# Attention scores on the two row halves of TensorE: head A on partitions 0-63, head B on 64-127

## The chip, the core and the metric

The kernel runs on one core of one Trainium2 chip. The metric is the time of one execution in device microseconds (us); for the kernel before, the median of three runs is 1126.16 us. Five engines work side by side and meet at semaphores: TensorE (PE in the profile, with PEld for its weight loads), VectorE (DVE), ScalarE (ACT), GpSimd (POOL) and SyncE (SP), which issues most DMA transfers.

## The reference

Three stages follow each other: an attention with a sigmoid in place of the softmax, a mixture of eight experts in which each token goes to the expert with the highest logit, and a feed-forward stage.

```python
scores = scale * np.matmul(q, k.transpose(0, 1, 3, 2)) - np.log(S)
attn = 1.0 / (1.0 + np.exp(-scores))
x = attn @ v                                     # 4 batches, 12 heads, S=448, D=64
logits = xn @ en.T / tau; expert = argmax(logits)
out[mask] = gate * (maximum(x[mask] @ w1[e], 0) @ w2[e])
h = out @ w_in;  result = (h - tanh(h)) @ w_out
```

The change touches only the scores of the attention.

## The kernel before

**Two parts for each float32.** Every large product is made from operands that are split into a high part in fp32r and the low rest, x = h + l, and summed from products of the parts.

**Units and slots.** Two heads, A and B, make a pair; there are 24 pairs, six for each batch. A unit is 128 keys by 448 queries of scores, put through the sigmoid and multiplied with v. 448 keys are three and a half times 128, so a pair has seven units: three of A, three of B, and one that holds the last 64 keys of A and of B. A slot is two units that follow each other; seven slots carry two pairs, and the middle one of the seven takes one unit of each pair. There are 84 slots, u = 0 to 83, and 21 of them make a batch.

**One slot.** `scores(u)` writes the two units into one of three PSUM buffers `pq` (two banks each). ACT reads it twice (L240 writes the high part `ah` of the sigmoid, L241 the full value back into `pq`), DVE subtracts (L242, `al`), and three slots later `av(u-3)` multiplies with v in three terms a unit (L255, six matmuls a slot). When all units of a pair are done, its result is copied (`xT`, L268 or L270) and `rows` turns it into token rows through a fourth user of the `pq` buffers (L280, `pr`).

**The scores before.** D is 64, so a head fills only 64 of the 128 partitions. The kernel therefore loads k and q twice, on partitions 0-63 and on 64-127 (`load`, L173). `prep` casts both (L192), then replaces q on the upper 64 partitions by its low part (L194, 64x448) and makes the low part of k (L196, 128x448). A matmul over 128 partitions then gives h·h and h·l at once, and a second one with k's low part gives the other two terms: two matmuls a unit, and four for the unit with the last keys, which takes A's and B's shares one after the other. That is 16 matmuls a pair. A and B have a tile each (`w[0]`, `w[1]`), so a pair has two casts, two L194 (A's on DVE, B's on POOL) and two L196 (POOL).

**What sets the order.** PE's program is written out by hand: scores(u), then av(u-3), then the events planned for slot u. `prep(i)` is planned for the slot after the last one of pair i-2, `load(i)` two slots after the last one of pair i-3, `rows(i)` five slots after the last one of pair i. The order on DVE, ACT, POOL and SP is made by a scheduler when the kernel is built; each engine then works its list strictly in order. `kq` has two buffers, so the load of pair i waits until DVE and POOL have read those of pair i-2.

**The end of the attention.** In batch 2 the routing of its tokens is planned eight slots after its rows, behind the scores of slot 75: `route_b` (L422, L424) ranks the tokens, POOL scatters the ids (L473), gathers ids and rows of the first group of tokens (L650, L654), ACT scales the rows (L658), and only after the rows does SP load the first expert's weights (L686), which ACT splits (L715) for the first matmuls of the experts (L725).

Of the kernel before, what the change touches and what calls it, by code (L numbers as in the profile page):

```python
# [10 lines left out]
F32 = mybir.dt.float32  # L11
F32R = mybir.dt.float32r
# [4 lines left out]
ALU = mybir.AluOpType  # L17
# [12 lines left out]
P = 128  # L30
# [4 lines left out]
def f32(ap):  # L35
    return ap.bitcast(F32)


class Prog:
# [87 lines left out]
    def attention(self):  # L127


        nc, tc = self.nc, self.tc  # L130
        B, H, S, D, NJ, E, R = self.B, self.H, self.S, self.D, self.NJ, self.E, self.R
        NP = H // 2
        HK = S - 3 * P
        cx = ExitStack()
        raw = self.pool("araw", 3, cx)
        sp = self.pool("asp", 3, cx)
        xp = self.pool("axp", 2, cx)
        pers = self.pool("apers", 1, cx)
        ps2 = self.pool("aps2", 3, cx, space=PSUM)
        self.ps1 = ps1 = ps2  # L140
        pav2 = self.pool("aps3", 2, cx, space=PSUM)

        self.ep = pers
        NV, NW = 2, 2
        ws, vhs, vls = [], [], []

        def wpads():
            for w in ws:
                for a, o in ((0, S), (1, 0)):
                    nc.gpsimd.memset(f32(w[a][:, 0::2, o : o + HK]), 0.0)  # L150

        def vpads():
            for i in range(NV):
                vh = pers.tile([P, 14, D], F32R, name=f"vh{i}")
                vl = pers.tile([P, 14, D], F32R, name=f"vl{i}")
                for t in (vh, vl):
                    nc.gpsimd.memset(f32(t), 0.0)
                vhs.append(vh)
                vls.append(vl)

        pairs = [(b, j) for b in range(B) for j in range(NP)]
        n = len(pairs)
        st = {}

        def load(i):

            b, j = pairs[i]
            kq = raw.tile([P, 2, 2, S], F32, tag="kq", name="kq", bufs=2)
            w = S if i == 0 else 2 * S
            for o in range(0, 2 * S, w):  # L170
                for t, src in ((1, self.q), (0, self.k)) if i == 0 else enumerate((self.k, self.q)):
                    for p0 in (0, D):
                        nc.sync.dma_start(  # L173
                            kq[p0 : p0 + D, t].rearrange("p a s -> p (a s)")[:, o : o + w],
                            src[b, j, :, o : o + w],
                        )
            vr = raw.tile([P, 2, 4, D], F32, tag="vr", name="vr")
            self.w_dma = nc.sync.dma_start(vr.rearrange("p h c d -> p (h c d)"), self.v[b, j])
            st[i] = dict(kq=kq, vr=vr)

        def prep(i):

            s = st[i]
            s["w"] = ws[i % NW]
            for a in range(2):
                kq = s["kq"][:, :, a]
                t = s["w"][a][:, :, a * HK : a * HK + S]
                if i == 0:
                    nc.vector.tensor_copy(t[:, 1], kq[:, 1])
                    nc.scalar.copy(t[:, 0], kq[:, 0])  # L190
                else:
                    nc.vector.tensor_copy(t[:, 0:2], kq)  # L192
                eng = nc.gpsimd if i and a else nc.vector
                eng.tensor_tensor(t[D:P, 1], kq[D:P, 1], f32(t[D:P, 1]), ALU.subtract)  # L194
                eng = nc.vector if i == 0 else nc.gpsimd
                eng.tensor_tensor(t[:, 2], kq[:, 0], f32(t[:, 0]), ALU.subtract)  # L196

        def prep_v(i):

# [6 lines left out]
            s["v"] = (vh, vl)  # L206


        units = []
        for i in range(n):  # L210
            units += [(i, 0, c * P, 8 + 2 * c) for c in range(3)]
            units += [(i, 2, 0, 6)]
            units += [(i, 1, (c + 1) * P, 2 * c) for c in range(3)]
        slots = [units[o : o + 2] for o in range(0, len(units), 2)]
        ns = len(slots)
        first = [7 * i // 2 for i in range(n)]
        final = [(7 * i + 6) // 2 for i in range(n)]
# [2 lines left out]
        def scores(u):  # L220
            hi = sp.tile([P, 2, S], F32R, tag="ah", name="ah", bufs=LAG + 2)
            lo = sp.tile([P, 2, S], F32R, tag="al", name="al", bufs=LAG + 2)
            tiles[u] = (hi, lo)
            pq = ps2.tile([P, 2, 512], F32, tag="qk", name="pq")
            for x, (i, a, c, _) in enumerate(slots[u]):
                w = st[i]["w"]
                ops = [(w[a], c)] if a < 2 else [(w[0], 3 * P), (w[1], 0)]
                m = 0
                for t, o in ops:
                    q = t[:, 1, :S] if t is w[0] else t[:, 1, HK:]  # L230
                    for z in (0, 2):
                        nc.tensor.matmul(  # L232
                            pq[:, x, :S], t[:, z, o : o + P], q, start=(m == 0), stop=(m == 2 * len(ops) - 1)
                        )
                        m += 1
            k = len(slots[u])
            pv = pq[:, :k, :S]
            sc = dict(bias=self.bias_s, scale=1.0 / math.sqrt(D))
            hi, lo = hi[:, :k], lo[:, :k]
            nc.scalar.activation(hi, pv, AF.Sigmoid, **sc)  # L240
            nc.scalar.activation(pv, pv, AF.Sigmoid, **sc)  # L241
            nc.vector.tensor_tensor(lo, pv, f32(hi), ALU.subtract)  # L242

        def av(u):
            hi, lo = tiles.pop(u)
            for x, (i, a, c, o) in enumerate(slots[u]):
                s = st[i]
                vh, vl = s["v"]
                if a == 0 and c == 0:
                    s["pav"] = pav2.tile([P, 512], F32, tag="av", name="pav")  # L250
                pav = s["pav"]
                vo = lambda t: t[:, o : o + 2].rearrange("p h d -> p (h d)")
                e = a == 1 and c == 3 * P
                for m, (vv, aa) in enumerate(((vh, hi), (vl, hi), (vh, lo))):
                    nc.tensor.matmul(  # L255
                        pav[:, :S], vo(vv), aa[:, x], start=(a == 0 and c == 0 and m == 0), stop=(e and m == 2)
                    )
                if e:
                    b, j = pairs[i]
                    if j == 0:  # L260
                        self.bts[b] = dict(
                            rec=xp.tile([CP, NCH, NJ * P], F32, tag="rec", name="rec"),
                            ss=self.sm.tile([CP, NCH], F32, tag="ss", name="ss"),
                            u=xp.tile([CP, NCH, E], F32, tag="u", name="u"),
                        )
                    s["xT"] = xp.tile([P, S], F32, tag="xT", name="xT")
                    if i % 2:
                        nc.scalar.copy(s["xT"], pav[:, :S])  # L268
                    else:
                        nc.vector.tensor_copy(s["xT"], pav[:, :S])  # L270
# [43 lines left out]

        self.bts = {}
        for i in range(NW):
            ws.append([pers.tile([P, 3, 512], F32R, name=f"w{i}{a}") for a in range(2)])
        wpads()
        vpads()
        with tc.high_priority():  # L320
            load(0)
            warm = self.cp.tile([P, 1], F32, name="warm")
            nc.scalar.activation(warm, self.bias_s, AF.Sigmoid)
        prep(0)
        for i in (1, 2):
            if i < n:
                load(i)
        if n > 1:
            prep(1)
        prep_v(0)  # L330
        pe = {mybir.EngineType.PE}
        with tc.manual_schedule(engines=pe):
# [29 lines left out]
            for i in range(n):  # L362
                if i >= 2:
                    plan(final[i - 2] + 1, prep, i)
                if i >= 3:
                    plan(final[i - 3] + 2, load, i)
                if i >= 1:
                    plan(first[i] + LAG - 2, prep_v, i)
                plan(final[i] + LAG + ROW + (3 if i == 0 else 0), rows, i)
                if pairs[i][1] == NJ - 1:  # L370
                    plan(final[i] + LAG + ROW, route, i)
            plan(5, self.embedding)
            now = [0]
            u = 0
            while u < ns + LAG:
                now[0] = u
                if u < ns:
                    scores(u)
                if LAG <= u < ns + LAG:
                    av(u - LAG)  # L380
                events(u)
                if u >= CONV:
                    conv()
                if u == ns and self.cv is not None:
                    for _ in self.cv:
                        pass
                u += 1
# [693 lines left out]
```

## Time and profile before

| what | value |
|---|---|
| median of 3 runs | 1126.16 us (1121.7 to 1127.59) |
| the profiled execution | 1122.56 us; span from first to last instruction 1120.8 us |
| PE busy over the span | 1030.4 us (92%), 6298 matmuls |
| DVE, ACT, POOL busy | 841.0 us (75%), 558.4 us (50%), 215.2 us (19%) |
| first sigmoid to routing of batch 2 | 10.40 us to 231.35 us |
| first matmul of the experts | 287.72 us |

The page gives busy time as an average over stages. A matmul of 448 columns is listed with some 365 ns, but the next one starts 0.20 us after it: matmuls overlap, and their starts, not their lengths, tell the rate. "[7.39 <-PE pq L232]" behind a row means that the engine sat idle for 7.39 us ahead of it and was released by line 232 on PE. "issue" stands where the profile names no releaser.

### The profile page before, as it was taken

How to read it: one execution, taken by the hardware profiler on the slowest of the kernel's cores; microseconds unless marked ns; L12 is line 12 of the kernel's file. 1: busy time of each engine (PE TensorE's matmuls, PEld its weight loads, DVE VectorE, ACT ScalarE, POOL GpSimd, SP SyncE). 2: the span in 40 equal slices, each digit the busy share in tenths (PEclk: the TensorE clock that was granted, in tenths of full speed). 3: DMA queues.
4: the chain of work that ended last, by engine and by line, in shares of the span. 5: the costliest groups of instructions: out<-in, count | busy, mean ns of one | idle time of the engine just before them, and what ended most of it. 6: DMA issues, size and time to landing. Idle time of an engine off the chain costs nothing. (4 is left out here: it accounts for less than half of the span.)

```text
span 1120.8 us, 16520 instructions
## 1 busy us (share of the span) xinstructions
PE 1030.4 (92%) x6298; PEld 980.6 (87%) x6298; DVE 841.0 (75%) x1136; ACT 558.4 (50%) x694; POOL 215.2 (19%) x218
## 2 busy tenths in 40 slices
PE   5998788892789999899999799999999999999996
PEld 4897687782779998899999799999999999999996
DVE  8999596790676977587888378888888666776674
ACT  4787576661556765566656353334435332233320
POOL 6666556451123111111000000000000210000002
PEclk8999899896799998899999899999999999999999
DMA  7675757606998899999683344454453442233312
GB/s 194 163 211 116 127 150 100 161 1 65 267 271 235 224 264 273 207 227 276 205 306 140 116 174 150 167 188 167 170 197 113 169 154 95 104 113 113 113 57 99
DMA packets 91800, 186.12 MB, mean 166 GB/s; under 512 B 13120, under 2 KB 64576, under 8 KB 91712
## 3 DMA queue, kind: packets, MB, share of 16 engines
q1 hardware_dynamic: 88064, 172.36, 54.6%
q0 software_dynamic: 3648, 12.61, 4.5%
q8 instruction: 52, 0.85, 0.3%
q14 instruction: 36, 0.29, 0.1%
HBM read 167.56 MB, written 36.26 MB: 182 GB/s over the span
## 5 line engine op out<-in xcount | busy, mean ns | idle before, releaser
L953 PE MATMUL o<-wo,gh 128*128 128x384 f32 x896 | 240.4, 335 | 0.7 <-DVE acc L963 0.7
L913 PE MATMUL z<-yh,wi 128*128 128x448 f32 x768 | 221.8, 371 | 6.0 <-ACT yh L888 6.0
L953 PEld LDWEIGHTS o<-wo,gh 128*128 128x128 f32 x896 | 162.9, 188 | 2.3 <-DVE acc L963 1.0
L913 PEld LDWEIGHTS z<-yh,wi 128*128 128x128 f32 x768 | 145.2, 190 | 18.4 <-ACT yh L888 6.2
L953 PE MATMUL o<-wo,gl 128*128 128x384 f32 x448 | 149.7, 334 | 0.0
L913 PE MATMUL z<-yl,wi 128*128 128x448 f32 x384 | 138.2, 368 | 0.0
L232 PE MATMUL pq<-w 128*128 128x448 f32 x384 | 101.8, 393 | 34.7 <-DVE al L242 22.5
L725 PE MATMUL pth<-xh,wh 128*128 128x256 f32 x432 | 124.3, 288 | 7.7 <-DVE hl L742 5.2
L725 PE MATMUL pty<-hh,wh 128*128 128x256 f32 x432 | 123.3, 290 | 6.1 <-ACT yT L758 4.1
L473 POOL DMA_INDIRECT out_dram<-acc,toki x14 | 17.3, 1232 | 578.6 <-DVE acc L963 578.6
L725 PE MATMUL pty<-hh,wl 128*128 128x256 f32 x432 | 123.6, 288 | 1.4 <-DVE wl L716 1.4
L725 PE MATMUL pth<-xl,wh 128*128 128x256 f32 x432 | 123.6, 286 | 0.0
L725 PE MATMUL pth<-xh,wl 128*128 128x256 f32 x432 | 123.3, 286 | 0.3 <-DVE wl L716 0.3
L725 PE MATMUL pty<-hl,wh 128*128 128x256 f32 x432 | 123.3, 287 | 0.0
L963 DVE TENSOR_TENSOR acc<-o,acc 128x768 f32<-128x768 f32 x98 | 93.5, 954 | 39.5 <-PE o L953 38.3
L240 ACT ACTIVATE ah<-pq,bias_s 128x896 fp32r<-128x896 f32 x84 | 85.0, 1012 | 66.3 <-PE pq L232 63.3
L232 PEld LDWEIGHTS pq<-w 128*128 128x128 f32 x384 | 73.4, 199 | 48.0 <-issue 32.2
L936 ACT CAST gh<-r 128x896 fp32r<-128x896 f32 x32 | 30.1, 941 | 158.7 <-DVE r L934 89.5
L242 DVE TENSOR_TENSOR al<-pq,ah 128x896 fp32r<-128x896 f32 x84 | 90.7, 1083 | 20.7 <-ACT pq L241 20.4
L716 DVE TENSOR_TENSOR wl<-w2raw,wh 128x1024 fp32r<-128x1024 f32 x54 | 66.2, 1225 | 34.2 <-ACT wh L715 33.3
L725 PEld LDWEIGHTS pth<-xh,wh 128*128 128x128 f32 x432 | 84.2, 195 | 8.2 <-issue 5.3
L725 PEld LDWEIGHTS pty<-hh,wh 128*128 128x128 f32 x432 | 84.0, 196 | 6.6 <-ACT yT L758 4.3
(199 smaller groups left out, 2206.0 us busy)
## 6 DMA issues: line engine op xcount, KB each, us to landing
w1raw<-in_moe_w_dram SPq DMA_DIRECT2D x36, 768.0 KB
w2raw<-in_moe_w_dram SPq DMA_DIRECT2D x27, 1024.0 KB
wi<-dwi SPq DMA_DIRECT2D x32, 768.0 KB
wo<-dwo SPq DMA_DIRECT2D x32, 768.0 KB
cr<-in_moe_w_in_dram SPq DMA_DIRECT2D x16, 768.0 KB
dwi<-cr SPq DMA_DIRECT2D x16, 768.0 KB
cr<-in_moe_w_out_dram SPq DMA_DIRECT2D x16, 768.0 KB
dwo<-cr SPq DMA_DIRECT2D x16, 768.0 KB
```

Of the source, the lines that this page charges most:

```text
L232: nc.tensor.matmul(pq[:, x, :S], t[:, z, o : o + P], q, start=(m == 0), stop=(m == 2 * len(ops) - 1))
L240: nc.scalar.activation(hi, pv, AF.Sigmoid, **sc)
L242: nc.vector.tensor_tensor(lo, pv, f32(hi), ALU.subtract)
L473: i = self.nc.gpsimd.indirect_dma_start(**kw)
L716: nc.vector.tensor_tensor(wl, cols, f32(wh), ALU.subtract)
L725: nc.tensor.matmul(pt[:, u], a[:, kk], b[:, kk], start=(n == 0), stop=(n == 3 * K - 1))
L913: nc.tensor.matmul(z[:, g, :GT], wi[:, a, j * P : (j + 1) * P], b[:, j], start=(n == 0), stop=(n == 3 * NJ - 1),)
L936: nc.scalar.copy(gv, r)
L953: nc.tensor.matmul(o[:, w, :NW], a[:, u, i * P : (i + 1) * P], wo[:, b, w * NW : (w + 1) * NW], start=(n == 0), stop=(n == 3 * CH - 1),)
L963: nc.vector.tensor_tensor(acc[i], ov, acc[i], ALU.add)
```

## The change

Head A lies on partitions 0-63 and head B on 64-127, each once. A tile `h` (high parts) and a tile `l` (low parts) hold, for both heads, 512 columns of k and 448 of q; the fourth block of 128 key columns is a block diagonal, with A's last 64 keys in its first 64 columns on the lower partitions, B's in its last 64 columns on the upper ones, and zeros elsewhere (`kpads` writes them once). A slot is now one A unit and one B unit with the same keys, and each unit is made of three matmuls over 64 partitions, h·h, h·l and l·h (the term l·l is left out), issued A, B, A, B, A, B. The middle slot of seven takes the block-diagonal unit of both pairs, three matmuls over all 128 partitions each. A pair has 18 matmuls over 64 partitions and 3 over 128. `prep` is one cast of 960 columns on DVE and two subtractions on POOL (448 and 512 columns). The load of a pair is five DMAs without copies, and `kq` has three fixed buffers in place of two.

```diff
-            kq = raw.tile([P, 2, 2, S], F32, tag="kq", name="kq", bufs=2)
...
+            kq = kqs[i % NK]
+            k, q = self.k[b, j], self.q[b, j]
+            for dst, src in (
+                (kq[:D, KW:], q[:, :S]),
+                (kq[D:, KW:], q[:, S:]),
+                (kq[:D, :S], k[:, :S]),
+                (kq[D:, : 3 * P], k[:, S + HK :]),
+                (kq[D:, S:KW], k[:, S : S + HK]),
+            ):
+                nc.sync.dma_start(dst, src)
...
-                    nc.vector.tensor_copy(t[:, 0:2], kq)
-                eng = nc.gpsimd if i and a else nc.vector
-                eng.tensor_tensor(t[D:P, 1], kq[D:P, 1], f32(t[D:P, 1]), ALU.subtract)
+                nc.vector.tensor_copy(h, kq)
+            for x in (qs, ks):
                 eng = nc.vector if i == 0 else nc.gpsimd
-                eng.tensor_tensor(t[:, 2], kq[:, 0], f32(t[:, 0]), ALU.subtract)
+                eng.tensor_tensor(l[:, x], kq[:, x], f32(h[:, x]), ALU.subtract)
...
+        slots = []
+        for i in range(0, n, 2):
+            ab = [[[(e, a, c * P, 8 * (1 - a) + 2 * c) for a in range(2)] for c in range(3)] for e in (i, i + 1)]
+            slots += ab[0] + [[(e, 2, 3 * P, 6) for e in (i, i + 1)]] + ab[1]
...
-                    for z in (0, 2):
-                        nc.tensor.matmul(
-                            pq[:, x, :S], t[:, z, o : o + P], q, start=(m == 0), stop=(m == 2 * len(ops) - 1)
-                        )
-                        m += 1
+            for m, (kt, qt) in enumerate(((0, 0), (0, 1), (1, 0))):
+                for x, (i, a, c, _) in enumerate(slots[u]):
+                    w = st[i]["w"]
+                    p = slice(0, P) if a == 2 else slice(a * D, (a + 1) * D)
+                    nc.tensor.matmul(
+                        pq[:, x, :S], w[kt][p, c : c + P], w[qt][p, KW:], start=(m == 0), stop=(m == 2)
+                    )
```

PE around slot 19, before: the last three products with v of slot 15, the rows of a pair, then the scores of slot 19 (`w_185` is A's tile, `w_186` B's, of pair 5; rows print the output's shape alone, so the height of a matmul in the array isn't seen).

```order
L255 MATMUL pav<-ah,vh_191 128x448
L255 MATMUL pav<-ah,vl_192 128x448
L255 MATMUL pav<-al,vh_191 128x448
L280 MATMUL pr<-ien,xT 112x136 x4
L232 MATMUL pq<-w_185 128x448 x2
L232 MATMUL pq<-w_186 128x448 x4
```

PE at the same place now (`w1h` and `w1l` are the high and low parts of pair 5).

```order
L253 MATMUL pav<-ah,vh_196 128x448
L253 MATMUL pav<-ah,vl_197 128x448
L253 MATMUL pav<-al,vh_196 128x448
L278 MATMUL pr<-ien,xT 112x136 x4
L230 MATMUL pq<-w1h 128x448 x2
L230 MATMUL pq<-w1l,w1h 128x448 x2
L230 MATMUL pq<-w1h,w1l 128x448 x2
```

Each "x2" is now A's matmul and B's with the same kind of term, on the two halves; every slot has six matmuls of scores where most had four.

DVE around slot 19, before: the subtractions `al` of slots 18 and 19 and, between them, the preparation of pair 7, with a cast for A, the low part of A's q, and a cast for B.

```order
L242 TENSOR_TENSOR al<-pq,ah 128x896
L192 CAST w_185<-kq 128x2x448
L194 TENSOR_TENSOR w_185<-kq,w_185 64x448
L192 CAST w_186<-kq 128x2x448
L242 TENSOR_TENSOR al<-pq,ah 128x896
L270 COPY xT<-pav 128x448
```

DVE at that place now, from `al` of slot 19 on.

```order
L239 TENSOR_TENSOR al<-pq,ah 128x896
L196 CAST w1h<-kq_188 128x960
L268 COPY xT<-pav 128x448
L207 CAST vh_196<-vr 128x4x64 x2
L239 TENSOR_TENSOR al<-pq,ah 128x896 x3
```

One cast is left of three operations; it waits for the last scores of the pair that used `w1h` before, and all of a pair's tile comes free at once, where A's came free ahead of B's.

More of the change, by code (lines that the diff above doesn't have):

```diff
@@ L143, in attention, with kpads @@
         self.ep = pers
[L144 to L150, printed above, removed]
+        NV, NW, NK = 2, 2, 3
+        KW = 4 * P
+        kqs, ws, vhs, vls = [], [], [], []
+        def kpads():
+            for t in kqs:
+                nc.vector.memset(t[:D, S:KW], 0.0)
+                nc.vector.memset(t[D:, 3 * P : S], 0.0)
         def vpads():
@@ L167, in load @@
             b, j = pairs[i]
-            kq = raw.tile([P, 2, 2, S], F32, tag="kq", name="kq", bufs=2)
[L169 to L175, printed above, removed]
-                        )
+            kq = kqs[i % NK]
[8 more added lines that the diff above has]
+                nc.sync.dma_start(dst, src)
             vr = raw.tile([P, 2, 4, D], F32, tag="vr", name="vr")
@@ L183, in prep @@
             s = st[i]
[L184 to L192, printed above, removed]
-                eng = nc.gpsimd if i and a else nc.vector
-                eng.tensor_tensor(t[D:P, 1], kq[D:P, 1], f32(t[D:P, 1]), ALU.subtract)
+            kq, (h, l) = s["kq"], ws[i % NW]
+            s["w"] = (h, l)
+            ks, qs = slice(0, KW), slice(KW, KW + S)
+            if i == 0:
+                nc.vector.tensor_copy(h[:, qs], kq[:, qs])
+                nc.scalar.copy(h[:, ks], kq[:, ks])
+            else:
+                nc.vector.tensor_copy(h, kq)
+            for x in (qs, ks):
                 eng = nc.vector if i == 0 else nc.gpsimd
-                eng.tensor_tensor(t[:, 2], kq[:, 0], f32(t[:, 0]), ALU.subtract)
+                eng.tensor_tensor(l[:, x], kq[:, x], f32(h[:, x]), ALU.subtract)
         def prep_v(i):
@@ L206, in prep_v @@
             s["v"] = (vh, vl)
[L209 to L214, printed above, removed]
+        slots = []
+        for i in range(0, n, 2):
+            ab = [[[(e, a, c * P, 8 * (1 - a) + 2 * c) for a in range(2)] for c in range(3)] for e in (i, i + 1)]
+            slots += ab[0] + [[(e, 2, 3 * P, 6) for e in (i, i + 1)]] + ab[1]
         ns = len(slots)
@@ L224, in scores @@
             pq = ps2.tile([P, 2, 512], F32, tag="qk", name="pq")
[L225 to L230, printed above, removed]
-                    for z in (0, 2):
-                        nc.tensor.matmul(
-                            pq[:, x, :S], t[:, z, o : o + P], q, start=(m == 0), stop=(m == 2 * len(ops) - 1)
-                        )
-                        m += 1
+            for m, (kt, qt) in enumerate(((0, 0), (0, 1), (1, 0))):
[5 more added lines that the diff above has]
+                    )
             k = len(slots[u])
@@ L248, in av @@
                 vh, vl = s["v"]
-                if a == 0 and c == 0:
-                    s["pav"] = pav2.tile([P, 512], F32, tag="av", name="pav")
+                if "pav" not in s:
+                    s["pav"], s["units"] = pav2.tile([P, 512], F32, tag="av", name="pav"), 0
                 pav = s["pav"]
                 vo = lambda t: t[:, o : o + 2].rearrange("p h d -> p (h d)")
-                e = a == 1 and c == 3 * P
+                b0, e = s["units"] == 0, s["units"] == 6
+                s["units"] += 1
                 for m, (vv, aa) in enumerate(((vh, hi), (vl, hi), (vh, lo))):
                     nc.tensor.matmul(
-                        pav[:, :S], vo(vv), aa[:, x], start=(a == 0 and c == 0 and m == 0), stop=(e and m == 2)
+                        pav[:, :S], vo(vv), aa[:, x], start=(b0 and m == 0), stop=(e and m == 2)
                     )
@@ L316, in attention @@
         for i in range(NW):
-            ws.append([pers.tile([P, 3, 512], F32R, name=f"w{i}{a}") for a in range(2)])
-        wpads()
+            ws.append([pers.tile([P, KW + S], F32R, name=f"w{i}{x}") for x in "hl"])
+        for i in range(NK):
+            kqs.append(pers.tile([P, KW + S], F32, name=f"kq{i}"))
+        kpads()
         vpads()
```

## The prediction, as it was written before the changed kernel ran

> **What bounds the kernel now.** I read the page first, for the span:
>
> ```profile
> span 1120.8 us, 16520 instructions
> ```
>
> The run took 1122.56 us, 1.8 us more than its span; the median of the three runs is 1126.16, so the profiled one is 0.3% below it, and I make the sum against 1122.56. Then the windows. The attention was cut at the sigmoids (L240) that open a batch of 21 slots, and the last piece starts at the routing of batch 2:
>
> ```profile
> core 0: us, PE busy (x) PEld busy (x) DVE busy (x) ACT busy (x) POOL busy (x), PEclk, DMA share, GB/s
> 10.40:66.96 56.56, 51.15 (x240) 44.31 (x240) 53.25 (x79) 42.23 (x48) 37.34 (x34) 0.94 0.71 189
> 66.96:122.00 55.04, 51.98 (x277) 47.20 (x276) 48.91 (x89) 43.69 (x56) 31.29 (x31) 1.00 0.68 133
> 122.00:186.26 64.26, 54.61 (x277) 48.66 (x276) 51.12 (x91) 43.93 (x56) 35.63 (x35) 0.95 0.67 135
> 186.26:231.35 45.09, 36.32 (x166) 31.82 (x164) 32.46 (x58) 27.86 (x38) 24.01 (x25) 0.89 0.51 134
> ```
>
> The second batch is the clean one: PE works 51.98 of 55.04 us, DVE 48.91, ACT 43.69. PE bounds it, with DVE close behind. What PE pays for a matmul is read from the starts in its timeline:
>
> ```profile
> 74.97 0.36 PE L255 MATMUL pav<-ah,vh 128*128 128x448 f32 x1
> 75.17 0.37 PE L255 MATMUL pav<-ah,vl 128*128 128x448 f32 x1
> 75.38 0.36 PE L255 MATMUL pav<-al,vh 128*128 128x448 f32 x1
> 75.58 0.97 PE L232 MATMUL pq<-w 128*128 128x448 f32 x4
> 76.39 0.36 PE L255 MATMUL pav<-ah,vh 128*128 128x448 f32 x1
> ```
>
> Seven starts in 1.42 us: 0.203 us each. The 96 score matmuls of a batch (16 for each of 6 pairs) are 19.5 us of PE.
>
> Batch three and the twelve slots behind it are slower than batch two, and the list of sigmoids shows one long gap in each, and a smaller one at the start:
>
> ```profile
> 10.40 1.01 ACT L240 ACTIVATE ah<-pq,bias_s 128x896 fp32r<-128x896 f32 x1 [4.47 <-PE pq L232]
> 14.49 1.01 ACT L240 ACTIVATE ah<-pq,bias_s 128x896 fp32r<-128x896 f32 x1 [1.74 <-PE pq L232]
> 135.83 1.01 ACT L240 ACTIVATE ah<-pq,bias_s 128x896 fp32r<-128x896 f32 x1 [7.39 <-PE pq L232]
> 199.06 1.01 ACT L240 ACTIVATE ah<-pq,bias_s 128x896 fp32r<-128x896 f32 x1 [7.51 <-PE pq L232]
> 230.40 1.01 ACT L240 ACTIVATE ah<-pq,bias_s 128x896 fp32r<-128x896 f32 x1 [2.12 <-PE pq L232]
> ```
>
> From the first row (slot 0) to the last (slot 75) are 75 slots. The first of the two long gaps, followed back:
>
> ```profile
> 124.80 1.14 POOL L196 TENSOR_TENSOR w<-kq,w 128x448 fp32r<-128x448 f32 x1
> 125.97 1.11 SPq L173 DMA_DIRECT2D kq<-in_k_dram  x2
> 132.13 0.63 DVE L192 CAST w<-kq 128x896 fp32r<-128x896 f32 x1 [6.26 <-DMA kq<-in_q_dram]
> 133.90 1.83 PE L232 MATMUL pq<-w 128*128 128x448 f32 x4 [5.27 <-DVE al L242]
> ...
> 195.36 0.63 DVE L192 CAST w<-kq 128x896 fp32r<-128x896 f32 x1 [6.34 <-DMA kq<-in_q_dram]
> ```
>
> POOL is done with `kq` at 125.94, the load of the pair two later goes out at 125.97, DVE sits in front of that pair's cast until 132.13, and `al`, which PE waits for, is queued behind the cast. The last row is the same wait in the second gap.
>
> Last, what follows slot 75:
>
> ```profile
> 231.35 0.19 PE L422 MATMUL prank<-oh,tri_b 112*128 112x32 bf16 x1
> 262.89 0.93 ACT L658 ACTIVATE xg<-xg 128x768 f32<-128x768 f32 x1 [12.60 <-DMA xg<-x_tok,gi]
> 286.83 1.56 ACT L715 CAST wh<-w1raw 128x768 fp32r<-128x768 f32 x2 [3.88 <-DMA w1raw<-in_moe_w_dram]
> ```
>
> From the routing at 231.35 a chain of scatters, gathers and weight loads runs 55.5 us to the experts' first cast, and ACT waits 12.60 us for the gathered rows; the last slots are done by then, or queued behind that wait. So a gain counts up to slot 75 alone, and moves everything behind it by as much. Of the 221 us ahead, that is 75/21 = 3.57 batches.
>
> **The change part by part.** *Scores on PE.* A batch has 54 pairs of half-height matmuls (9 for each of 6 pairs of heads) and 18 full ones, 3.65 us. What two halves cost together no row shows. They have 448 columns each, and PE's rate goes by columns (256 pass in 0.120 us in the next rows), so less than one full matmul, 0.203 us, is excluded: that is the lower end. If both run at once they still need two weight loads, and the experts' matmuls of 256 columns bring a load with each; behind them the lengths of this kernel's score matmuls and loads, and a load beside the matmul ahead of it:
>
> ```profile
> 400.05 0.28 PE L725 MATMUL pty<-hl,wh 128*128 128x256 f32 x1
> 400.17 0.28 PE L725 MATMUL pty<-hh,wl 128*128 128x256 f32 x1
> 400.29 0.28 PE L725 MATMUL pty<-hh,wh 128*128 128x256 f32 x1
> ...
> L232 PEld LDWEIGHTS pq<-w x384: 186/188/338, 8.3 to 249.8; 128*128 128x128 f32 x192
> L232 PE MATMUL pq<-w x384: 358/366/743, 8.3 to 250.0; 128*128 128x448 f32 x192
> ...
> 60.09 0.37 PE L255 MATMUL pav<-ah,vl 128*128 128x448 f32 x1
> 60.09 0.19 PEld L255 LDWEIGHTS pav<-al,vh 128*128 128x128 f32 x1
> ```
>
> A load and its matmul pass every 0.120 us, so two loads take at most 0.240 us. I take 0.22, between the two: 54 x 0.22 = 11.9, with the full ones 15.5 us, 4.0 less than 19.5. The Trainium skill (TensorE: Matmul & The Clock Gate, Part 3 on packing small matmuls) models tiles on different rows as running at once, a few ns apart; a pair would then be an estimated 0.207 us and the sum 1093. No row of this case shows it.
>
> *Changes of height.* 18 of 21 slots now go from full height (products with v) to half and back, 36 changes a batch. If the array runs on, each costs 0; if the next matmul can start only when the last has left, it costs what a matmul lasts beyond its pace, 0.366 - 0.203 = 0.163 us. A gain has no reason. Nothing is nearer to either end, so I take half, 0.08: 2.9 us. PE's net is -1.1 us a batch, x 3.57 = -3.9 us.
>
> *Preparation.* The operations of the second batch:
>
> ```profile
> L192 DVE CAST w<-kq 128x896 fp32r<-128x896 f32 x12 | 8.0, 669 | 2.2 <-PE pav L255 2.0
> L194 DVE TENSOR_TENSOR w<-kq,w 64x448 fp32r<-64x448 f32 x6 | 5.9, 991 | 0.2
> L196 POOL TENSOR_TENSOR w<-kq,w 128x448 fp32r<-128x448 f32 x10 | 11.5, 1149 | 5.9 <-DVE w L192 5.5
> PE pq L232 <- DVE al L242: 3.0, 3, 2.1
> PEld pq L232 <- DVE al L242: 0.9, 1, 0.9
> ```
>
> DVE loses 8.0 + 5.9 and gains six casts of 960 columns, by length 0.72 us each, 4.3: 9.6 of its 48.91 us go. PE's waits for `al` in this batch are 3.9 us. All could go or none; PE's own pace holds some slots to the same time. I take half, 1.95 x 3.57 = -7.0 us, between 0 and -13.9. On POOL two subtractions a pair, 1.15 and by length 1.31 us, take the place of three. The new cast waits for the last scores of pair i-2, with `al` of the next slot queued behind it, but that `al` needs the same scores through ACT, so the wait costs nothing. Cast and subtractions are 0.72 + 1.15 + 1.31 = 3.2 us; three slots at 55.04/21 = 2.6 us each cover them. Were that cover gone, PE would wait the rest, up to 3 us a pair.
>
> *Loads.* The third `kq` buffer ties a load to the pair three before, one pair (3.5 slots, 9 us) earlier than now, against a wait of 6.26; and a pair is half the data:
>
> ```profile
> kq<-in_k_dram SPq DMA_DIRECT2D x46, 224.0 KB
> ```
>
> Four such DMAs a pair were 896 KB, now 448. SP issues six DMAs a pair with v's in place of five, some 0.6 us each (1.11 for two above), 3.5 us in 9. Both long gaps should go: -7.4 - 7.5 = -14.9 us; what is late next is PE itself. At the start head B's separate preparation (the 1.74) goes too: -1.7. The six memsets of `kpads` come before the first `kq` lands, when DVE is idle (0.87 us in the next row), and the ones on POOL go; if they took longer than that, some tenths.
>
> ```profile
> 4.14 3.36 DVE L189 CAST w<-kq 128x448 fp32r<-128x448 f32 x1 [0.87 <-DMA kq<-in_q_dram]
> ```
>
> *Sum.* -3.9 - 7.0 - 14.9 - 1.7 = -27.5: 1122.6 - 27.5 = **1095 us**. With both ends of each term (-17.4 to +10.6 for PE, 0 to -13.9 for the waits) this case spans 1075 to 1117. ACT, with 43.69 us a batch, doesn't bind even at the low end: 55.04 - 4.9 - 3.9 = 46.2.
>
> **The rivals.** *The halves take turns (slower).* If the second half starts only when the first has passed, a pair costs 2 x 0.203, 54 of them 21.9 us, and PE's net is 21.9 + 3.65 - 19.5 + 2.9 = +9.0 a batch, +32.1; with -23.6 for the rest, 1131 (1121 with free changes of height, 1141 with the dear ones). It is over 0.5% slower once a change of height costs over 0.06 us. For it: in every row of before a matmul starts a whole pace after the last. Against it: all of those use all 128 rows, so they had to.
>
> *Changes of height are dear.* The halves run at once, but the array empties at each change, and the next weights are loaded only then: 0.163 to 0.163 + 0.188 = 0.35 us a change, +1.9 to +8.6 a batch, 1106 to 1130, the middle 1118. For it: a weight load of 188 ns starts with the matmul before it, and may have nowhere to go while that runs at another height. Against it: before shows no change of height at all. The Trainium skill (TensorEngine Tiling (Array Packing), Key Properties) says that changing the tiling mode drains TensorE. By that rule alone the sum is this case's lower end, 1106; no row of this case shows it.
>
> *The gaps stay.* If the loads are held up by POOL's slow readings after the routing, as now, and a third buffer only moves the gap, the 14.9 come back: 1110. Against it: the wait is shorter than the pair gained.
>
> **How the numbers follow.** 0.5%, 5.6 us, is about what a measurement can tell from no change: faster is below 1117, slower above 1128. The forecast case has 0.55, all faster; dear changes 0.19 (0.10 faster, 0.06 same, 0.03 slower); turns 0.17 (0.05 same, 0.12 slower); the gaps 0.09 (0.08 and 0.01). Together 0.73 faster, 0.12 same, 0.15 slower. The range goes from near the low end of the forecast case, 1076, to 1125, and leaves out most of the turns, the worst of the dear changes and the edge of the forecast case: under 0.2.
>
> **What would show it.** Right: in PE's timeline the starts of A's and B's half in one group lie far closer than 0.2 us, three such pairs take 0.6 to 0.72 us, and the first product with v follows with at most 0.16 us more; no row of a cast of `w` waits for `kq` for long; DVE near 39 us in a clean batch, the routing near 204 us, the first expert cast 55 us later. Wrong: halves 0.2 us apart (turns); idle or late starts of 0.2 us and more where height changes; a gap of 6 us ahead of a cast; or a routing that comes earlier while the experts don't.

## The result, and the profile after

The changed kernel takes 1098.45 us, median of four runs (1097.49 to 1100.32), beside 1125.79 us for the kernel before (four runs, 1121.7 to 1127.59): a ratio of 0.975, 95% interval 0.972 to 0.978. The forecast was 1095 us in a range from 1076 to 1125. The profiled execution took 1099.0 us.

The page of the kernel after gives the span, and the windows cut the attention at the same points as before: the first sigmoid (now L237) of each batch, and the routing of batch 2.

```profile
span 1097.3 us, 16753 instructions
```

```profile
core 0: us, PE busy (x) PEld busy (x) DVE busy (x) ACT busy (x) POOL busy (x), PEclk, DMA share, GB/s
8.84:60.86 52.02, 48.72 (x269) 36.08 (x268) 42.76 (x64) 41.53 (x47) 25.81 (x26) 1.00 0.49 145
60.86:115.26 54.40, 53.12 (x306) 40.91 (x307) 44.60 (x78) 43.95 (x56) 28.29 (x30) 1.00 0.44 106
115.26:169.75 54.49, 53.15 (x306) 40.92 (x307) 44.95 (x78) 43.96 (x56) 28.01 (x30) 1.00 0.45 106
169.75:203.00 33.25, 31.92 (x182) 24.94 (x182) 29.12 (x48) 27.67 (x38) 15.65 (x17) 1.00 0.32 93
```

Piece by piece against before: the start comes 1.6 us earlier (10.40 to 8.84), the batches are 4.5, 0.6 and 9.8 us shorter, and the last piece, up to the routing at 203.14, is 11.7 us shorter (45.09 to 33.39; its row stops at 203.00). The clean second batch, which was to show what the new scores are worth, has gained almost nothing: 55.04 to 54.40 us. Two more columns moved. The granted clock is 1.00 in every piece, where before it was 0.94, 0.95 and 0.89 in three of the four; and the DMA share in a clean batch fell from 0.68 to 0.44.

One slot in PE's timeline of the kernel after, its scores and the first of its products with v. "x2" is A's half and B's half under one start:

```profile
69.92 0.47 PE L230 MATMUL pq<-w1h 64*128 64x448 f32 x2
70.23 0.37 PE L230 MATMUL pq<-w1l,w1h 64*128 64x448 f32 x2
70.44 0.36 PE L230 MATMUL pq<-w1h,w1l 64*128 64x448 f32 x2
70.73 0.47 PE L253 MATMUL pav<-ah,vh 128*128 128x448 f32 x1
71.03 0.37 PE L253 MATMUL pav<-ah,vl 128*128 128x448 f32 x1
71.24 0.36 PE L253 MATMUL pav<-al,vh 128*128 128x448 f32 x1
```

Where nothing changes height, starts lie 0.20 to 0.21 us apart, and that holds for a pair of halves as for one full matmul. At a change they don't: 0.31 us behind the first pair, 0.29 from the last pair to the first product, 0.30 behind that product. PE's weight loads at the second of these places:

```profile
70.23 0.19 PEld L230 LDWEIGHTS pq<-w1h,w1l 64*128 64x128 f32 x2
70.73 0.19 PEld L253 LDWEIGHTS pav<-ah,vh 128*128 128x128 f32 x1 [0.30 <-issue]
70.84 0.19 PEld L253 LDWEIGHTS pav<-ah,vl 128*128 128x128 f32 x1
```

The load for the first product of the other height starts at 70.73, with its own matmul, and the next load 0.11 us later; where the height stays, a load starts with the matmul ahead of its own, as the first of these rows does. Two intervals of some 0.1 us beyond the pace stand around each change, 0.2 us in all.

Behind the attention, in the timelines of PE and ACT after:

```profile
203.14 0.19 PE L422 MATMUL prank<-oh,tri_b 112*128 112x32 bf16 x1
...
254.48 0.83 ACT L715 CAST wh<-w1raw 128x768 fp32r<-128x768 f32 x1 [3.90 <-DMA w1raw<-in_moe_w_dram]
```

The routing comes 28.2 us earlier (231.35), the experts' first cast 32.35 us (286.83), but the span is only 23.5 us shorter. The experts' stage, from that cast to the last copy of their result (L758), as one window of before and one of after:

```profile
286.83:632.14 345.31, 331.16 (x2693) 329.01 (x2693) 260.53 (x356) 208.09 (x282) 45.65 (x33) 0.97 0.88 234
```

```profile
254.48:610.04 355.56, 333.27 (x2693) 330.64 (x2693) 259.84 (x356) 207.66 (x282) 47.06 (x33) 0.96 0.88 227
```

It has the same 2693 matmuls and moves as much (345.31 us x 234 GB/s and 355.56 x 227 are both some 81 MB), and is 10.25 us longer. The balance: -28.2 to the routing, -4.1 from there to the first cast, +10.25 in the experts, -1.4 in the feed-forward stage (488.66 to 487.26), together -23.5.

### The profile page after: what moved, and what is told of

The parts are those of the page before. It is cut to its first block, busy times and chain, and to the rows that moved or that the text cites. A ratio compares the mean times of both kernels' runs of the same rounds, so it can differ in the third digit from the quotient of the medians.

```text
span 1097.3 us, 16753 instructions
## 1 busy us (share of the span) xinstructions
PE 1028.9 (94%) x6418; PEld 952.1 (87%) x6418; DVE 816.6 (74%) x1093; ACT 557.7 (51%) x693; POOL 185.5 (17%) x191
## 5 line engine op out<-in xcount | busy, mean ns | idle before, releaser
L237 ACT ACTIVATE ah<-pq,bias_s 128x896 fp32r<-128x896 f32 x84 | 85.4, 1016 | 41.2 <-PE pq L230 39.8
L725 PEld LDWEIGHTS pth<-xh,wh 128*128 128x128 f32 x432 | 86.1, 199 | 18.8 <-issue 14.2
L716 DVE TENSOR_TENSOR wl<-w1raw,wh 128x768 fp32r<-128x768 f32 x72 | 68.6, 956 | 31.6 <-ACT wh L715 31.1
L725 PEld LDWEIGHTS pth<-xh,wl 128*128 128x128 f32 x432 | 85.8, 199 | 1.9 <-DVE wl L716 1.9
L715 ACT CAST wh<-w2raw 128x1024 fp32r<-128x1024 f32 x54 | 56.5, 1048 | 58.9 <-PE pty L725 24.4
```

Of the source, the lines that this page charges most:

```text
L715: nc.scalar.copy(wh, cols)
L716: nc.vector.tensor_tensor(wl, cols, f32(wh), ALU.subtract)
L725: nc.tensor.matmul(pt[:, u], a[:, kk], b[:, kk], start=(n == 0), stop=(n == 3 * K - 1))
```

## The experiments

The theory at the start: the third kq buffer had removed the two gaps; the halves run at the same time; each change of height costs 0.2 us and eats what the halves save; the experts' stage lost 10 us because its transfers come in another order. The runs were made on three other chips. The kernel before takes longer there (medians 1142.01, 1144.04 and 1143.72 us), the changed one too (1114.31 us on one of them, ratio 0.975, 0.971 to 0.980), so totals are compared as ratios to the kernel before on the same chip. The changed kernel's attention takes nearly the same time on the one of them where it ran (routing at 204.9 us in place of 203.1), so places in it can be compared in microseconds. The kernel before is less steady.

### The buffer or the bytes

The kernel before with one more buffer:

```diff
-            kq = raw.tile([P, 2, 2, S], F32, tag="kq", name="kq", bufs=2)
+            kq = raw.tile([P, 2, 2, S], F32, tag="kq", name="kq", bufs=3)
```

> The kernel before with a third kq buffer and nothing else. Theory (the two gaps came from the second buffer falling free too late, and the third buffer of the change removed them): no cast waits for kq, both gaps of 7.39 and 7.51 us go, the routing comes at 231.35 - 14.9 = 216.5 us, and the time is 1111 us, or up to 10 us more if the experts' stage gives time back as it did after the change (345.3 to 355.6 us). Rival (the gaps went because the change halves the bytes of kq, whatever the buffers): the gaps stay, routing near 231 us, time near 1126 us.

The changed kernel with one fewer:

```diff
-        NV, NW, NK = 2, 2, 3
+        NV, NW, NK = 2, 2, 2
```

> The changed kernel with two kq buffers in place of three. Theory (the buffer did it): a cast waits for kq again once a batch, about half as long as before because half the bytes come, 3 to 4 us each, 7 us in all: routing near 210 us, time near 1105 us. Rival (half the bytes did it): no cast waits for kq, routing stays near 203 us and the time near 1098 us.

DVE's waits for kq in the kernel before with a third buffer, and, below, in the kernel before as it is on another of these chips:

```profile
DVE w L192 <- DMA kq<-in_q_dram: 0.5, 1, 0.5
```

```profile
DVE w L192 <- DMA kq<-in_q_dram: 14.8, 3, 8.8
```

The buffer alone ends the waits and brings the routing to 222.8 us, 8.6 us ahead of the profiled run of before (15.4 ahead of the 238.2 us on that other chip). The changed kernel with two buffers has its routing at 203.06 us, as with three, at a ratio of 0.972 (0.965 to 0.978). So the third buffer alone is enough, and the rest of the change alone is enough: the theory was wrong in giving the third buffer all the credit. That half the bytes did it doesn't follow either, since the traces show another thing that the change moved, the time from the first DMA of a pair's load to its first cast. For the pair of the first gap it was 6.2 us in the kernel before (125.97 to 132.13), 16.3 with the third buffer (109.6 to 126.0), and in the changed kernel 15.8 with two buffers (107.6 to 123.4) and 21.8 with three (101.8 to 123.6). The second gap has 6.3 us before. In the kernel before, this load waits for POOL's last reading of the pair two earlier, done at 125.94, 18.4 us after that pair's first cast (107.59); in the changed kernel with two buffers it goes out 1.9 us after that pair's only cast (105.7). One cast and two subtractions read a pair's `kq` now, in place of two casts and four subtractions, so a buffer comes free sooner. What the smaller transfers add to this no run tells apart. The first run had a surprise as well. Its ratio is 1.003 (1.000 to 1.006): its experts' stage took 379.3 us, and nothing of the earlier routing was left.

### Do the halves run at the same time?

The changed kernel with A's three terms first and then B's:

```diff
-            for m, (kt, qt) in enumerate(((0, 0), (0, 1), (1, 0))):
-                for x, (i, a, c, _) in enumerate(slots[u]):
+            for x, (i, a, c, _) in enumerate(slots[u]):
+                for m, (kt, qt) in enumerate(((0, 0), (0, 1), (1, 0))):
```

> The changed kernel with the score matmuls of a slot in the order A, A, A, B, B, B in place of A, B in turns. Theory (the two halves run at the same time, a pair in 0.205 us): only the last A and the first B still overlap, five passes in place of three, 2 x 0.203 = 0.41 us more for each of 18 slots a batch, 7.3 us a batch, 26 us over 3.57 batches: routing near 229 us, time near 1124 us. Rival (the halves take turns, and the 0.205 us is a reading of merged records): the order changes nothing, 1098 us.

Its PE timeline at the same slot:

```profile
69.83 0.48 PE L230 MATMUL pq<-w1h 64*128 64x448 f32 x2
70.14 0.38 PE L230 MATMUL pq<-w1l,w1h 64*128 64x448 f32 x2
70.34 0.37 PE L230 MATMUL pq<-w1h,w1l 64*128 64x448 f32 x2
```

The order makes next to no difference: routing at 204.20 us, ratio 0.976 (0.970 to 0.982). The rows stand in the order of their starts, and each "x2" is A's and B's matmul of the same term: B's first started before A's second, though A's three are issued ahead of all of B's. (That the order was built so is seen in the slots of full height, where the tiles' names tell the two apart: there the three terms of `w0` pass ahead of the three of `w1`.) But this alone doesn't tell whether the halves overlap, since a half-high matmul might take half the time. So the next kernel puts both on the same rows (it computes A's scores twice and leaves out B's):

```diff
-                    p = slice(0, P) if a == 2 else slice(a * D, (a + 1) * D)
+                    p = slice(0, P) if a == 2 else slice(0, D)
```

> The changed kernel with both score matmuls of a pair put on rows 0 to 63 (the scores of head B are left out: head A's rows stand in for them). The same number, shape and order of matmuls. The run with A, A, A, B, B, B left the time where it was, so either the halves run side by side whatever the order, or a half-high matmul by itself takes only half the time. Theory (side by side): on the same rows they must follow each other, a pair takes 0.41 us in place of 0.205, 0.61 us more in each of 18 slots a batch, 39 us over 3.57 batches: routing near 242 us. Rival (a half-high matmul takes 0.10 us): no change, routing near 203 us.

Its PE timeline:

```profile
70.11 0.67 PE L230 MATMUL pq<-w0h 64*128 64x448 f32 x2
70.62 0.57 PE L230 MATMUL pq<-w0l,w0h 64*128 64x448 f32 x2
71.03 0.57 PE L230 MATMUL pq<-w0h,w0l 64*128 64x448 f32 x2
71.52 0.47 PE L253 MATMUL pav<-ah,vh 128*128 128x448 f32 x1
```

On the same rows a pair takes 0.41 us. From the first pair to the first product are 1.41 us, against 0.81 in the changed kernel, the routing comes at 238.4 us (242 expected; the changed kernel has 5.5 us of waits of its scores for `al`, which can absorb some of it), and the ratio is 1.002 (0.999 to 1.006). So the halves run side by side, and this saving is real; without it the change would have been worth nothing.

### What a change of height costs

The changed kernel with the three score pairs set between the pairs of products, six changes a slot in place of two (`s3` and `a6` are the same matmuls as lists):

```diff
-                    scores(u)
...
-                    av(u - LAG)
+                    for m in range(3):
+                        s3[m]()
+                        a6[2 * m]()
+                        a6[2 * m + 1]()
```

> The changed kernel with the three score pairs of a slot put between the pairs of matmuls of the other product, so that the height of the tiles changes 6 times in a slot in place of 2; the same matmuls. Theory (each change of height costs about 0.2 us of TensorE): 4 x 0.2 = 0.8 us more in 18 of 21 slots, 14.4 us a batch, 51 us over 3.57 batches: routing near 254 us, time near 1150 us. Rival (the change of height is cheap, 0.08 us as the prediction took, and the rest of a slot's 0.4 us is a wait for the slot's own data): 20 us more, 1119 us, or nothing if even that is hidden.

```profile
73.08 0.47 PE L236 MATMUL pq<-w0h,w0l 64*128 64x448 f32 x2
73.48 0.47 PE L269 MATMUL pav<-ah,vl 128*128 128x448 f32 x1
73.79 0.37 PE L269 MATMUL pav<-al,vh 128*128 128x448 f32 x1
74.09 0.47 PE L236 MATMUL pq<-w0h 64*128 64x448 f32 x2
```

A round of three passes and two changes takes 1.01 us, where three passes at the pace take 0.61: again 0.20 us a change. The routing went to 247.5 us, 44.3 later, over 18/21 x 75 = 64 slots with four more changes each 0.17 us a change; the waits of PE's scores for `al`, 5.5 us in the changed kernel, are down to 1.2. The ratio is 1.008 (1.005 to 1.012), 0.8% longer than the kernel before. The theory holds, the 0.08 of the prediction doesn't.

### Two ways to have fewer changes

Scores of two slots together, then the products of two (`two` holds both slot numbers):

```diff
-                if u < ns:
-                    scores(u)
-                if LAG <= u < ns + LAG:
-                    av(u - LAG)
+                for x in two:
+                    if x < ns:
+                        scores(x)
+                for x in two:
+                    if x >= LAG:
+                        av(x - LAG)
```

> The changed kernel with the scores of two slots issued together and then the other product of two slots, so that the height changes 2 times in two slots in place of 4. Theory (0.2 us a change, and TensorE bounds the attention): 0.4 us less for two slots, 3.6 us a batch, 13 us over 3.57 batches: routing near 190 us, time near 1085 us. Rival (the burst of two slots' scores leaves TensorE waiting for the score buffers, of which there are few, and for the exponentials): the waits take the 0.4 us back and more, 1098 us or slower.

The events planned for the two slots (loads, preparations, rows) now come together as well, behind the products. The changes are halved, and the routing comes 10 us later, at 213.1 us; ratio 0.983 (0.978 to 0.988). PE now waits where it hadn't (7.9 us for `al`, 7.3 behind `t`, L122, on DVE), and after the waits the clock falls, in the windows of this kernel:

```profile
80.00:90.00 10.00, 7.62 (x44) 6.07 (x42) 7.37 (x10) 10.00 (x15) 5.33 (x6) 1.00 0.25 68
90.00:100.00 10.00, 8.52 (x47) 7.09 (x48) 7.58 (x22) 4.09 (x7) 1.12 (x2) 0.83 0.21 54
```

The second way keeps every product with v in halves, too, on two banks that are added at the end of a pair; the scores give up a buffer for it:

```diff
-        ps2 = self.pool("aps2", 3, cx, space=PSUM)
+        ps2 = self.pool("aps2", 2, cx, space=PSUM)
...
+                    for g in range(2):
+                        p = slice(g * D, (g + 1) * D)
                         nc.tensor.matmul(
-                            pav[:, :S], vo(vv), aa[:, x], start=(b0 and m == 0), stop=(e and m == 2)
+                            pav[:, g, :S], vo(vv)[p], aa[p, x], start=(b0 and m == 0), stop=(e and m == 2)
```

> The changed kernel with the second product, too, in halves of 64 rows: each matmul of 128 keys becomes two of 64 that go to two banks and are added at the end of a head pair, so that the height changes only at the block diagonal, 2 times in 7 slots in place of 12. It needs two more banks, so the scores have two buffers in place of three. Theory (0.4 us a slot for two changes, TensorE bounds the attention): 10 changes of 0.2 us less in 7 slots, 6 us a batch, 21 us over 3.57 batches: routing near 182 us at best, 190 us with some waits for the score buffers. Rival (two score buffers are too few, TensorE waits for al in each slot): routing at 203 us or later.

```profile
69.90 0.38 PE L255 MATMUL pav<-al,vh 64*128 64x448 f32 x2
70.10 0.38 PE L230 MATMUL pq<-w1h 64*128 64x448 f32 x2
70.30 0.38 PE L230 MATMUL pq<-w1l,w1h 64*128 64x448 f32 x2
70.51 0.38 PE L230 MATMUL pq<-w1h,w1l 64*128 64x448 f32 x2
70.71 0.37 PE L255 MATMUL pav<-ah,vh 64*128 64x448 f32 x2
```

Between scores and products of the same height the pace isn't broken, 0.20 us at every start. So it is the height, and not the other tile or line, that costs. But PE's waits in this kernel are long; its row up to 200 us, and the same row of the changed kernel up to its routing:

```profile
PE pq L230 <- DVE al L239: 37.2, 29, 8.0
```

```profile
PE pq L230 <- DVE al L239: 5.5, 5, 1.3
```

The routing comes at 250.35 us, ratio 1.011 (1.004 to 1.018). That fits the rival, two score buffers are too few, but it isn't shown apart from the additions at the end of a pair, which are new as well; what this version would give with three buffers was not tried, for want of banks.

### The experts' stage

Fewer of the conversion's transfers in each group of the experts, in the changed kernel and in the one before:

```diff
-CPG, CPF = 6, 2
+CPG, CPF = 3, 2
```

> The changed kernel with the conversion's transfers of the experts' stage cut to 3 in a group of matmuls in place of 6, so that they are spread over twice as many groups. Theory (the 10 us that the experts' stage gave back, 345.3 to 355.6 us, are waits for weights behind these transfers in the groups where the DMA engines are full, and an evener spread avoids them): no group above 40 us, the stage at 345 us or less, time near 1088 us. Rival (the stage is bound by the bytes it moves, whatever the order): 355 us stays, 1098 us.

> The kernel before with the same cut from 6 to 3 transfers in a group. Theory (queue order costs the kernel before less in the experts' stage, 42.34 and 42.57 us groups among ones of 36): its stage falls from 345.3 us to some 335 us, time near 1116 us. Rival (bound by bytes): no change, 1126 us.

And more of that work early, in the attention:

```diff
-NEARLY, NFFN = 1, 8
+NEARLY, NFFN = 4, 8
```

> The changed kernel with the number of early conversion transfers in the attention raised from 1 to 4. In the attention the DMA engines are busy 0.45 of the time, in the experts' long groups all of it. Theory (the experts' stage loses its 10 us to bytes that could move earlier): the stage falls by the time of the bytes moved ahead, to 350 us or less, and the routing stays near 203 us: 1093 us or less. Rival (the early transfers stand ahead of the loads of kq on their queue and delay the casts): routing later by some us, no gain, 1098 us or slower.

Spreading did nothing for the changed kernel (stage 365.3 us, ratio 0.969, 0.963 to 0.975, an interval that overlaps the changed kernel's own) and made the one before 1% longer (375.4 us, 1.010, 1.006 to 1.013). The early work comes with a stage of 358.6 us but brought the routing to 213.0; ratio 0.975 (0.970 to 0.979). Its arithmetic goes to DVE, 50.00 us busy in the second window of this kernel against 44.60; that this is what delays the routing is likely, but was not tried apart:

```profile
60.86:115.26 54.40, 47.33 (x260) 35.79 (x260) 50.00 (x82) 41.49 (x54) 27.48 (x25) 0.97 0.53 139
```

Last, both kernels once more, on one chip, each with a profile:

> The changed kernel once more, beside the kernel before on the same chip, with a profile of each. Theory (the experts' stage gives back some 10 us because its transfers come in another order): it is longer here too than in the kernel before, by 5 to 15 us. Rival (the stage is bound by its bytes and its length differs from run to run and chip to chip by as much): the difference is under 5 us or has the other sign.

> The kernel before once more on the same chip. Both theories: routing at 231 us with the two waits of a cast for kq of 7 to 8 us, since the attention runs at the full granted clock; the experts' stage is what differs, by either theory as told for the other run.

The stage as a window of before, and of after:

```profile
297.99:658.69 360.70, 335.01 (x2693) 332.89 (x2693) 260.75 (x356) 208.48 (x283) 45.80 (x33) 0.95 0.90 224
```

```profile
257.76:622.11 364.35, 338.35 (x2693) 334.90 (x2693) 259.74 (x356) 207.50 (x283) 45.91 (x33) 0.95 0.88 222
```

The kernel before has its routing at 238.2 us here, 7 later than expected, with waits for kq of 8.77 and 5.11 us. The stage's difference is 3.65 us, under the 5 that was set. The same stage takes 345 to 379 us in the runs of the kernel before and its variants, 356 to 370 in those of the changed one, with 81 MB in each of them but the one with early work (76 MB). So the 10 us of the first pair of profiles are not a fixed price of the change, and no edit to the order won them back. What sets the length within that spread stays open. For the 379.3 us of the kernel before with three kq buffers, a part can be read in ACT's timeline:

```profile
324.94 0.89 ACT L813 ACTIVATE ca<-cr 128x768 f32<-128x768 f32 x1 [15.95 <-DMA cr<-in_moe_w_out_dram]
```

ACT sits 15.95 us in front of a transfer of the conversion, and the copy of the experts' result (L758), which PE needs, is queued behind it. PE waits 14.2 us there; in the two profiles of the kernel before its waits for that copy are 4.1 and 2.2 us in all. Why the transfer came so late isn't shown.

## Why the prediction came out, step by step

The time was within 3.5 us of the forecast and the routing within 1 us (203.85 by the sum, 203.14 measured), but by luck. Up to the routing, PE's program and its waits were to give 10.9 us and gave 2.3; the gaps were to give 14.9 and gave 20.5; start and batch one were to give 1.7 and gave 5.5. These errors nearly cancel, 27.5 us forecast and 28.2 measured, and 4.7 us were lost behind the routing, for which there was no term.

**Pair of halves.** Forecast 0.22 us, measured 0.205: the two run at once, as shown by putting them on the same rows. The estimate by the packing rule of the Trainium skill (TensorE: Matmul & The Clock Gate, Part 3), 0.207 us, was the nearer one. 54 pairs are 11.1 us, with the full ones 14.7, 4.8 less than before.

**Changes of height.** Forecast 0.08 us, measured 0.20. This is the step that failed: "Nothing is nearer to either end, so I take half" put the cost between nothing and a drain, when the runs show two late starts of some 0.1 us at each change: that of the first matmul at the new height, and that of the matmul behind it, since the first one's load isn't pulled ahead. The rival "changes of height are dear" was right in that. The drain that the Trainium skill states (TensorEngine Tiling (Array Packing), Key Properties) agrees with the trace so far as a change costs time; that the array empties wholly the trace doesn't show, since the first product starts 0.29 us behind the last pair, which is listed with 0.36. 36 changes are 7.2 us a batch, so PE's net by count is -4.8 + 7.2 = +2.4 us, where -1.1 was forecast; PE's busy time rose by 1.14 us. The scores in halves did not make PE's program shorter.

**Waits for DVE.** Forecast -1.95 us a batch; PE's time outside its busy time in the clean batch went from 3.06 to 1.28 us, -1.78: the size is right. The reason given for it is shown only in part: DVE's own busy time was forecast near 39 us and is 44.60, 4.3 less than before in place of 9.6, and a PE that has more to do may wait less by itself. The casts and subtractions of kq went from 13.9 to 3.9 us, as worked out, but the casts of v take longer, for a reason that no run shows. The groups of DVE in the clean batch of before and of after:

```profile
L204 DVE CAST vh<-vr 128x256 fp32r<-128x256 f32 x12 | 6.1, 504 | 0.5 <-PE pav L255 0.4
```

```profile
L207 DVE CAST vh<-vr 128x256 fp32r<-128x256 f32 x13 | 8.9, 706 | 1.0 <-PE pav L253 0.3 <-POOL vl L208 0.3 <-issue 0.3
```

PE and waits together were to give -10.9 us over 3.57 batches; the clean batch gives -0.64 x 3.57 = -2.3.

**The gaps.** Forecast -14.9 us; batch three gained 9.13 more than a clean batch and the last piece 11.33, so -20.5. Both waits went, as they go with the third buffer alone and without it. What was missed stands in the windows that the prediction itself quotes: 0.94, 0.95 and 0.89 as the granted clock of the pieces with gaps. After such a wait PE runs at half speed for a while. Two windows of before behind the first gap, 4 us each:

```profile
134.00:138.00 4.00, 4.00 (x11) 3.61 (x12) 2.43 (x5) 1.88 (x2) 0.73 (x1) 0.52 0.60 147
138.00:142.00 4.00, 4.00 (x22) 3.69 (x22) 3.58 (x4) 3.51 (x5) 2.85 (x3) 1.00 1.00 316
```

11 matmuls pass in the first, 22 in the second. In PE's timeline of before the same is seen behind the second gap, starts 0.375 us apart until 202.50, and 0.20 from 202.80 on:

```profile
197.13 1.83 PE L232 MATMUL pq<-w 128*128 128x448 f32 x4 [5.42 <-DVE al L242]
198.76 0.58 PE L255 MATMUL pav<-ah,vh 128*128 128x448 f32 x1
199.13 0.58 PE L255 MATMUL pav<-ah,vl 128*128 128x448 f32 x1
...
202.50 0.47 PE L255 MATMUL pav<-ah,vh 128*128 128x448 f32 x1
202.80 0.36 PE L255 MATMUL pav<-ah,vl 128*128 128x448 f32 x1
```

14 passes at 0.172 us more each are 2.4 us behind this gap, 10 are 1.7 behind the first. What of it came before the sigmoid is counted in the waits of 7.39 and 7.51 already (four scores each, 0.7 us). A third stretch stands in the last piece, behind a wait of 2.07 us of PE:

```profile
219.77:223.18 3.41, 3.41 (x11) 3.01 (x10) 1.42 (x5) 1.89 (x3) 1.04 (x1) 0.50 0.18 50
```

Nine passes at half clock, 1.5 us. The two waits (14.9), what of the first two stretches isn't in them (2.7) and this one are 19.1 of the 20.5 us; the rest is not accounted for.

**The start and batch one.** The forecast's 1.7 us is the wait of 1.74 ahead of the second sigmoid, at 14.49, which lies in batch one, not ahead of it. The start is 1.6 us earlier for another reason, which no term had: PE's first scores begin at 6.89 us in place of 8.30. Batch one gained 3.9 us beyond a clean batch. The gain lies ahead of its fifth sigmoid, the first row in before, the second in after:

```profile
21.71 1.01 ACT L240 ACTIVATE ah<-pq,bias_s 128x896 fp32r<-128x896 f32 x1 [1.75 <-PE pq L232]
```

```profile
16.08 1.01 ACT L237 ACTIVATE ah<-pq,bias_s 128x896 fp32r<-128x896 f32 x1
```

From the first sigmoid to the fifth are 11.31 us before and 7.24 after, 4.1 less. The wait of 1.74 is gone, and so is one of 1.75, behind a stretch at half clock in the windows of before:

```profile
16.00:20.00 4.00, 3.34 (x10) 2.84 (x10) 3.97 (x5) 3.96 (x5) 3.84 (x5) 0.50 0.95 239
```

Ten matmuls pass in it at 0.172 us more each, 1.7 us. The forecast had the first of these two waits, and not the second. The column doesn't show all: at the very start the passes of the changed kernel, too, start 0.37 us apart (8.60 to 10.46), with PEclk at 1.00 there.

**The tail.** "Moves everything behind it by as much" held for the routing's chain roughly (51.3 us in place of 55.5) and failed for the experts: +4.7 us in all of what is behind the routing. 1122.56 - 28.2 + 4.7 = 1099.0, the time of the profiled run.

**The rivals.** Halves in turns: refuted. Height changes dear: right that a change costs more than 0.163 us, at 0.20 near its low end; the kernel still gained because the gaps and the half clock behind them were worth more. The gaps stay: refuted.

## What to carry to other kernels

Read PEclk in every window in which PE waits, and the starts of the matmuls at the beginning of a kernel, where it doesn't show the half pace: a wait of 5 us cost its own length and some 2 us of half-speed matmuls behind it, and a change that removes the wait wins both. Packing two half-height products side by side saves 0.2 us a pair against running them in turns, and each alternation with full-height work costs 0.2 us, so count the changes before counting the pairs. Grouping work of one height should save changes, but in both versions tried here the waits for buffers and operands cost more than it saved. An earlier start of a stage that lives on transfers is not all won: measure to the end of that stage.

## What the runs showed of the hardware that was not expected

- The two row halves do not only overlap, they need not be issued in turns: with A, A, A, B, B, B the six matmuls take the same three passes. The packing rule of the Trainium skill (TensorE: Matmul & The Clock Gate, Part 3) has matmuls start in the order of the program; here a matmul of the other rows started ahead of two that were issued before it, and the routing differed by 1.1 us where 26 were expected of strict order.
- A change of height costs 0.20 us for matmuls of 448 columns, some 0.1 before and 0.1 behind the first one at the new height, whichever way it goes; its weight load starts with it and not one matmul ahead.
- In the kernel before, PE idle for 5.3 to 5.4 us was followed by 3.9 and 5.4 us at half clock, at 0.375 us a matmul; in the changed kernel's first profile, where no wait of PE in the attention is longer than 1.5 us, the granted clock stayed at 1.00. Between these lengths it can go either way. Three times in the kernel before, PE's starts lay 2.33 to 2.35 us apart (behind 88.8, 153.1 and 217.0 us), and only the last was followed by half clock. In the changed kernel's profile on the other chip, a wait of 1.65 us was enough:

```profile
39.40:42.80 3.40, 3.40 (x12) 2.18 (x11) 2.46 (x5) 2.60 (x4) 0.00 (x0) 0.50 0.00 0
```
